# One attention and two MLPs on one core: the first MLP's weights loaded in step with their conversion, and chunk 1's Y transposed earlier

## The chip, the cores and the metric

One core of a Trainium2 chip runs the whole program in one launch. The metric is device time in microseconds (us). Engines are named as in the profile: PE (TensorE, with PEld for its weight loads), DVE (VectorE), ACT (ScalarE), POOL (GpSimd) and SP (SyncE, which here only issues DMAs).

## The reference

The inputs are q, k and v (4 x 8 x 768 x 48, float32), beta, and weights that reach the chip as 8-byte floats.

```python
for t in range(S):                       # per batch and head, k normalized
    y[:, :, t] = q[:, :, t] @ state      # read before the update
    state += beta[t] * outer(k[t], v[t] - state.T @ k[t])
x = y as 3072 x 384
h = x @ w_in                             # 384 x 2048
x = (max(h, 0) + alpha * min(h, 0)) @ w_out          # 2048 x 384
out = (silu(x @ w_gate) * (x @ w_val)) @ w_out2      # 384 x 1536, 1536 x 384
```

## The kernel before

**Stages.** The 768 time steps are cut into 24 chunks of 32. Attention of a chunk gives 128 rows of x (32 steps of 4 batches). The first MLP takes two chunks as one block (256 columns, 16 inner slices j, functions `H1`, `H1_parts`, `O1`), the second takes three. A `prelude` (lines 830 to 925) does chunks 0 and 1 by hand; everything after it is a list of events, each with a time in units, sorted and issued in that order. Each engine executes its own instructions in the order in which the program issued them.

**Attention.** `pre_T` transposes k or q on PE (ACT or DVE copies it out), `pre_G` makes the products of k and q, `lanes2(0)` inverts a triangular matrix for chunks 0 to 3, mostly on DVE. It begins with `norm` (line 218), whose first instruction is a square root on ACT (line 222) that DVE waits for. Then follow for each chunk `do_KS`, `do_QS`, `do_U`, `do_S`, `do_Y` and `do_XT`: small matmuls with one copy or sum behind each. `do_Y` copies Y out on ACT (`ys`, line 475); `do_XT` transposes it on PE and ACT and DVE write its two parts (`xh`, `xl`, lines 491 and 492). `H1` of block 0 needs `do_XT` of chunks 0 and 1.

**Weights of the first MLP.** There are 32 slices, 384 KB each; even ones are from w_in, odd ones from w_out. Each slice has a home in SBUF. `Slice.load` issues its DMA on SP. `all_w1` (line 797) is a generator that converts the slices, three steps for each slice: at step z=0 of slice i ACT reads slice i+2 (line 519, this waits for that slice's DMA), DVE does the first of three bit operations on slice i (lines 527, 529, 533, one a step), and ACT copies the upper part of slice i-1 (line 540). At z=1 the lower part of slice i-1 is subtracted (line 541), on POOL for the first 16 slices. The converted halves are written over the home of the slice. The float32 form lives in 8 tiles that the x tiles lend at first, then in 4 rotating ones, each free after the subtraction. `go(conv, n)` runs n steps: 3, then `C_A` = 6, `C_B` = 8, `C_C` = 9, 3, 3, `C_D` = 7, 2, 3 and 3 in the prelude, 47 steps in all; 50 more are events spread over units -0.5 to 13.5 of block 0.

**SP's queue before.** In this order: k of window 0 (4 DMAs), slices 0 to 4, q of window 0 (4), slice 5, k of window 1 (4), alpha, k of chunk 0 (4), slices 6 to 11, beta, slices 12 to 15, k of chunk 1, q of window 1 (waits for PE to have read k of window 1), slices 16 to 25, v of chunk 2, slices 26 to 31. None of the slices waits for the conversion.

Of the kernel before, what the change touches and what calls it, by code (L numbers as in the profile page):

```python
# [8 lines left out]
F32 = mybir.dt.float32  # L9
# [15 lines left out]
def kernel(  # L25
# [25 lines left out]
    nc = tc.nc  # L51
# [8 lines left out]
    J1 = FF1 // 128  # L60
# [5 lines left out]
    NB2 = NCH // CB2  # L66
    LA = 2
    W1_DVE = 16
    W64 = 1
    WF = 4  # L70

# [28 lines left out]
    def load_nat(w, nm, to, eng=nc.sync):  # L100

        src = {"k": k, "q": q}[nm]
        for b in range(4):
            eng.dma_start(
                out=to[b // 2][:, :, b % 2, 0:D],
                in_=src[b, :, w * 128:w * 128 + 128, :].rearrange("h t d -> t h d"),
            )
# [3 lines left out]
    def load_beta(w, eng=nc.sync):  # L111
        t = ap.tile([128, C], F32, name="beta", tag="beta", bufs=1)
        for b in range(4):
            eng.dma_start(
                out=t[32 * b:32 * b + 32],
                in_=beta[b, :, w * 4 * C:(w + 1) * 4 * C].rearrange("h (c t) -> c h t", c=4),
            )
        beta_t[w] = t
# [5 lines left out]
    def load_k2(c, eng=nc.sync):  # L124
        load_steps(k2_t[c % 2][:, 0 : H * D].rearrange("p (h d) -> p h d", h=H), k, c, eng)
# [3 lines left out]
    def load_v(c, eng=nc.sync):  # L129
        t = ap.tile([128, H, D], F32, name="v", tag="v", bufs=2)  # L130
        load_steps(t, v, c, eng)
        v_t[c] = t
# [7 lines left out]
    def bank(early, name):  # L140
        pool, tag = (ps_h1, "h1") if early else (ps_a, "a")
        return pool.tile([128, 512], F32, name=name, tag=tag)
# [272 lines left out]
    def do_QS(c):  # L415
        y_ps[c] = ps_y.tile([128, 512], F32, name="py", tag="y")
        if c > 0:
            state_rows(y_ps[c], c, 1, False)
# [61 lines left out]
    def do_XT(c):  # L480
        n, ci = divmod(c, 2)
        if ci == 0:
            x1_t[n] = [x1.tile([128, NK, N1], F32R, name=f"x{s}", tag=f"x{s}") for s in ("h", "l")]
        xh, xl = x1_t[n]
        ys = ys_t.pop(c)
        ps = bank(False, "px")
        for kk in range(NK):
            nc.tensor.transpose(ps[:, kk * 128:kk * 128 + 128], ys[:, kk * 128:kk * 128 + 128], ident)
        pv = ps[:, 0:NK * 128].rearrange("p (k t) -> p k t", k=NK)
        cs = slice(ci * 128, ci * 128 + 128)  # L490
        nc.scalar.activation(out=xh[:, :, cs], in_=pv, func=AF.Copy)  # L491
        nc.vector.tensor_tensor(xl[:, :, cs], pv, xh[:, :, cs], ALU.subtract)  # L492


    class Slice:
# [8 lines left out]
        def load(self, eng=nc.sync):  # L504
# [3 lines left out]
            else:  # L508
                if self.home is None:
                    w = wstg.tile([128, 384], I64, name="w64", tag="w64", bufs=W64)  # L510
                else:
# [25 lines left out]
    def split(f, eng, pool, tag):  # L537

        t = pool.tile([128, 2, 384], F32R, name="w", tag=tag, **({} if pool is ws else dict(bufs=1)))
        nc.scalar.activation(out=t[:, 0], in_=f, func=AF.Copy)  # L540
        return t, lambda: eng.tensor_tensor(t[:, 1], f, t[:, 0], ALU.subtract)  # L541
# [9 lines left out]
    for s in ("h", "l", "h", "l"):  # L551
        t = x1.tile([128, NK, N1], F32, name="ef" + s, tag="x" + s).rearrange("p k t -> p (k t)")
# [3 lines left out]
    def w1_slice(i):  # L556
        j, z = divmod(i, 2)
        src, parts = (w_rows(moe_w_out, j), 1) if z else (w_cols(moe_w_in, j), NK)

        wide = src.dtype == I64  # L560
        return Slice(src, parts, ws.tile([128, 384], I64, name="w64", tag="w") if wide else None)

    w1_s = [w1_slice(i) for i in range(2 * J1)]
# [222 lines left out]
    def warm(n, t=ident[:, 0:96]):  # L786

        if not warm_t:
            warm_t.append(ps_o1.tile([128, 2, 512], F32, name="warm", tag="o1"))
        for _ in range(n):  # L790
            nc.tensor.matmul(warm_t[0][0:96, 0, 0:96], t, t, start=True, stop=True)

    def load_w1(*slices, eng=nc.sync):
        for i in slices:
            w1_s[i].load(eng)

    def all_w1():


        n = 2 * J1  # L800
        rest = None
        for i in range(-2, n + 1):
            if i + 2 < n:
                w1_s[i + 2].act()
            if i < 0:
                continue
            for z in range(3):
                if i < n:
                    w1_s[i].dve(z)
                if z == 0 and i > 0:  # L810
                    t, rest = split(w1_s[i - 1].f, nc.vector if i >= W1_DVE and i % 2 else nc.gpsimd, ws, "w")
                    w1.append(t)
                if z == 1 and rest:
                    rest()
                if i < n or z == 1:
                    yield

    conv = all_w1()

    def go(g, n=1):  # L820
        for _ in range(n):
            next(g, None)
# [7 lines left out]
    def prelude():  # L830
        nc.vector.memset(St[:, 0, 0:2, :], 0.0)
        for z in range(2):
            nc.vector.memset(nat[z][:, :, :, D:64], 0.0)
        for z in range(2):
            nc.vector.memset(k2_t[z][:, H * D :], 0.0)
        nc.vector.memset(mask[:, 0:1], 1.0)
        nc.scalar.activation(out=mask[:, 1:2], in_=mask[:, 0:1], func=AF.Sqrt)
        make_identity(nc, ident)
        for z in range(2):
            nc.gpsimd.memset(natq0[z][:, :, :, D:64], 0.0)  # L840
        nc.gpsimd.memset(mask, 1.0)
        for g in range(4):
            m = mask[32 * g:32 * g + 32, :]
            nc.gpsimd.affine_select(
                out=m, in_=m, pattern=[[1, C]], compare_op=ALU.is_gt, fill=0.0, base=0, channel_multiplier=-1
            )
        load_nat(0, "k", nat)
        load_w1(0, 1, 2, 3, 4)
        load_beta(0, nc.gpsimd)
        load_v(0, nc.gpsimd)  # L850
        load_v(1, nc.gpsimd)
        warm(4, St[:, 0, 0:2, :].rearrange("p h e -> p (h e)"))
        n = 0
        for b1 in range(2):
            for half in range(2):
                pre_T(0, "k", b1, half, nat, early=n % 2 == 1, eng="act" if n % 2 == 0 else "dve")
                n += 1
        load_nat(0, "q", natq0)
        load_w1(5)
        load_nat(1, "k", nat)  # L860
        nc.sync.dma_start(out=alpha_r, in_=moe_alpha.rearrange("(j p) -> j p", p=128))
        load_k2(0)
        load_w1(*range(6, 12))
        go(conv, 3)
        for c in range(4):
            pre_G(c, (0,), early=c % 2 == 1)
        go(conv, C_A)
        inv = lanes2(0, True)
        go(inv, 3)
        load_beta(1)  # L870
        n = 0
        for b1 in range(2):
            for half in range(2):
                pre_T(0, "q", b1, half, natq0, early=n % 2 == 1)
                n += 1
        go(inv, 6)
        pre_G(0, (1,))
        go(inv, 2)
        pre_G(1, (1,), early=True)
        pa = bank(False, "pal")  # L880
        nc.tensor.transpose(pa[:, 0:J1], alpha_r, ident[0:J1, 0:J1])

        c = slope[:, 0]
        nc.vector.tensor_scalar(c, pa[:, 0:J1], -1.0, 1.0, op0=ALU.mult, op1=ALU.add)
        nc.vector.tensor_scalar(slope[:, 1], c, 0.0, 2.0, op0=ALU.is_ge, op1=ALU.mult)
        nc.vector.tensor_scalar(slope[:, 1], slope[:, 1], -1.0, None, op0=ALU.add)
        nc.vector.tensor_tensor(c, c, slope[:, 1], ALU.mult)
        nc.vector.tensor_scalar(c, c, -1.0, None, op0=ALU.mult)
        go(inv, 2)
        scale_v(0)  # L890
        scale_v(1)
        for b1 in range(2):
            for half in range(2):
                pre_T(1, "k", b1, half, nat)
        load_w1(*range(12, 16))
        load_k2(1)
        load_nat(1, "q", nat)
        load_w1(*range(16, 26))
        warm(6)
        go(inv, 7)  # L900
        go(inv)
        go(conv, C_B)
        go(inv)
        do_QS(0)
        do_U(0)
        go(conv, C_C)
        do_S(0)
        load_v(2)
        load_w1(*range(26, 2 * J1))
        go(conv, 3)  # L910
        do_KS(1)
        go(conv, 3)
        do_Y(0)
        do_QS(1)
        do_U(1)
        go(conv, C_D)
        do_XT(0)
        go(conv, 2)
        do_Y(1)
        go(conv, 3)  # L920
        do_S(1)
        load_k2(2)
        go(conv, 3)
        do_XT(1)
        return inv

    def base(c):
# [7 lines left out]
    for w in range(1, NWIN):  # L935
        P = base(4 * w) - 32
        if w == 1:
# [8 lines left out]
            l0, l1, n = 11.8, 23.6, LANES  # L946
        else:
# [9 lines left out]
            l0, l1, n = P + 15, P + 31.5, LANES  # L957
# [115 lines left out]
```

## Time and profile before

| | |
|---|---|
| device time, three runs | 1125.52, 1126.56 (median), 1130.23 us |
| profiled execution | span 1123.7 us from first to last instruction; its own device time is not listed beside it |
| busy | PE 1069.2, DVE 612.2, ACT 412.1, POOL 338.2 us |
| mean granted TensorE clock | 0.971 |
| moved by DMA | 76.40 MB, of which instructions 2.06 MB on one queue (126 packets) and 0.28 MB on another |

The page cuts the span into 40 slices of 28 us; a digit is a busy share in tenths. A row of a timeline is: start, duration, engine, line, operation, output and inputs, count, and in brackets how long the engine was idle before it and what released it ("issue": nothing that the profile shows). The chain of waits lists start and duration of the work that ended last.

### The profile page before, as it was taken

Reading aid. Unit: us, or ns where it says so; the run is one execution under the profiler, and the core shown is the slowest. Engines: PE = TensorE matmul, PEld = TensorE weight load, DVE = VectorE, ACT = ScalarE, POOL = GpSimd, SP = SyncE. Lnnn points to the kernel's source line nnn. Section 1 sums busy time; section 2 is a strip of 40 time slices with the busy share of each in tenths; the row PEclk is TensorE's granted clock in tenths of the full one; section 3 lists DMA queues with packets and bytes.
Section 4 is the critical chain, followed back from the end, with each engine's and each line's share of the span. In section 5 each row is a group of like instructions: output and inputs, shape, how many; then the busy total and the mean of one; then the engine's idle time right before and its main releaser. Section 6 shows DMA issues by size and latency. Waiting matters only on the chain.

```text
span 1123.7 us, 36882 instructions
## 1 busy us (share of the span) xinstructions
PE 1069.2 (95%) x16125; PEld 1038.2 (92%) x16125; DVE 612.2 (54%) x1314; ACT 412.1 (37%) x965; POOL 338.2 (30%) x521
## 2 busy tenths in 40 slices
PE   5559899999999999999999999999999999999998
PEld 4549788999999999999998999999999999999998
DVE  5867983974795497469544354433333333333333
ACT  3346343345434434533433564322222222222222
POOL 4334562742473274347322452100000000000000
PEclk8569999999999999999999999999999999999999
DMA  9941032405334240521333343010101010101000
GB/s 198 294 134 32 11 73 66 95 13 140 89 59 119 83 95 21 152 68 31 93 101 103 116 138 92 2 41 2 42 1 42 1 42 2 42 1 42 1 22 22
DMA packets 140196, 76.40 MB, mean 68 GB/s; under 512 B 104036, under 2 KB 134788, under 8 KB 140036
## 3 DMA queue, kind: packets, MB, share of 16 engines
q1 hardware_dynamic: 139460, 73.45, 25.3%
q8 instruction: 126, 2.06, 0.8%
q0 software_dynamic: 384, 0.41, 0.1%
q14 instruction: 34, 0.28, 0.1%
q10 hardware_dynamic: 192, 0.20, 0.1%
HBM read 57.52 MB, written 16.52 MB: 66 GB/s over the span
## 4 chain that ended last, share of the span: by engine, by line
PE 85%; DVE 6%; issue 4%; DMA 2%; ACT 1%; POOL 1%; SPq 0%; DVEq 0%; ACTq 0%; POOLq 0%
PE gv L696 27%; PE o L637 17%; PE h L606 16%; PE o L726 13%; PE pg L171 2%; PE pst L445 2%; PE pk L400 1%; PE pu L426 1%; PE pt L152 1%; PE py L466 1%; PE py L400 1%; POOL w L541 1%; DVE X L269 1%; DMA w<-in_moe_w_val_dram 1%; DMA w<-in_moe_w_out_dram 1%
## 5 line engine op out<-in xcount | busy, mean ns | idle before, releaser
L696 PE MATMUL gv<-x2s,w 128*128 128x384 f32 x1728 | 316.4, 335 | 0.0
L696 PEld LDWEIGHTS gv<-x2s,w 128*128 128x128 f32 x1728 | 303.2, 188 | 0.0
L606 PE MATMUL h<-xh,w 128*128 128x256 f32 x1152 | 242.5, 287 | 9.6 <-DVE pn L617 5.2
L637 PE MATMUL o<-gh,w 128*128 128x256 f32 x1728 | 247.6, 289 | 0.1
L626 POOL TENSOR_TENSOR gh<-pn,gh 128x256 fp32r<-128x256 f32 x192 | 155.3, 809 | 284.7 <-ACT gh L625 231.4
L637 PEld LDWEIGHTS o<-gh,w 128*128 128x128 f32 x1728 | 218.5, 190 | 5.4 <-DVE xs L652 0.3
L606 PEld LDWEIGHTS h<-xh,w 128*128 128x128 f32 x1152 | 193.0, 191 | 12.7 <-ACT xh L491 5.7
L606 PE MATMUL h<-xl,w 128*128 128x256 f32 x576 | 164.0, 285 | 2.6 <-DVE xl L492 2.6
L726 PE MATMUL o<-w,us 128*128 128x384 f32 x864 | 165.0, 336 | 0.0
L617 DVE SCALAR_TENSOR_TENSOR pn<-pn,slope,h 128x256 f32<-128x256 f32 x192 | 91.2, 475 | 121.2 <-ACT pn L616 120.8
L726 PEld LDWEIGHTS o<-w,us 128*128 128x128 f32 x864 | 151.2, 188 | 0.0
L708 DVE TENSOR_TENSOR sg<-sg,gv 128x384 f32<-128x384 f32 x96 | 53.2, 554 | 166.4 <-ACT sg L706 166.4
L625 ACT ACTIVATE gh<-pn 128x256 fp32r<-128x256 f32 x192 | 80.0, 417 | 131.2 <-DVE pn L617 129.7
L616 ACT ACTIVATE pn<-h,slope 128x256 f32<-128x256 f32 x192 | 90.0, 469 | 84.8 <-PE h L606 84.4
L606 PEld LDWEIGHTS h<-xl,w 128*128 128x128 f32 x576 | 110.3, 192 | 3.5 <-DVE xl L492 3.5
L681 POOL TENSOR_TENSOR x2s<-x2r,x2s 128x384 fp32r<-128x384 f32 x21 | 21.0, 1029 | 307.5 <-ACT x2s L679 307.5
L713 ACT ACTIVATE us<-u 128x384 fp32r<-128x384 f32 x96 | 50.5, 526 | 164.7 <-DVE u L709 164.7
L706 ACT ACTIVATE sg<-gv 128x384 f32<-128x384 f32 x96 | 47.3, 492 | 160.2 <-PE gv L696 160.1
L714 DVE TENSOR_TENSOR us<-u,us 128x384 fp32r<-128x384 f32 x96 | 53.6, 559 | 62.5 <-ACT us L713 62.5
L709 DVE TENSOR_TENSOR u<-sg,gv 128x384 f32<-128x384 f32 x96 | 53.2, 554 | 46.1 <-PE gv L696 46.1
L269 DVE TENSOR_TENSOR X<-X,tmp 128x31 f32<-128x31 f32 (+29 forms) x155 | 68.1, 439 | 4.8
L519 ACT ACTIVATE wf<-w 128x384 f32<-128x384 f32 x60 | 33.1, 552 | 84.4 <-DMA w<-in_moe_w_out_dram 27.3
(116 smaller groups left out, 1012.5 us busy)
## 6 DMA issues: line engine op xcount, KB each, us to landing
w<-in_moe_w_out_dram SPq DMA_DIRECT2D x28, 384.0 KB
w2d<-wf SPq DMA_DIRECT2D x36, 192.0 KB
wf<-w2d SPq DMA_DIRECT2D x36, 192.0 KB
w<-in_moe_w_in_dram SPq DMA_DIRECT2D x16, 384.0 KB
nat<-in_k_dram SPq DMA_DIRECT2D x24, 192.0 KB
k<-in_k_dram SPq DMA_DIRECT2D x96, 48.0 KB
x2d<-xs SPq DMA_DIRECT2D x12, 384.0 KB
w<-in_moe_w_gate_dram SPq DMA_DIRECT2D x12, 384.0 KB
```

What stands on the lines that cost most here:

```text
L269: eng.tensor_tensor(Xv, Xv, w, ALU.subtract)
L606: nc.tensor.matmul(ps[:, 0:N1], w[:, a, kk * 128:kk * 128 + 128], x[b][:, kk, :], start=(i == 0), stop=(i == 3 * NK - 1),)
L616: nc.scalar.activation(out=g, in_=hv, func=AF.Relu, scale=slope[:, 0, j:j + 1])
L617: nc.vector.scalar_tensor_tensor(out=g, in0=g, scalar=slope[:, 1, j:j + 1], in1=hv, op0=ALU.mult, op1=ALU.add)
L625: nc.scalar.activation(out=gh[:, 0], in_=g, func=AF.Copy)
L626: nc.gpsimd.tensor_tensor(gh[:, 1], g, gh[:, 0], ALU.subtract)
L637: nc.tensor.matmul(o[:, dm // 2, (dm % 2) * N1:(dm % 2) * N1 + N1], w[:, a, dm * 128:dm * 128 + 128], g[:, b], start=(j == 0 and i == 0 an ...
L696: nc.tensor.matmul(p[:, 0:N2], w2[j, z][:, a, kk * 128:kk * 128 + 128], x[:, b, kk], start=(i == 0), stop=(i == 3 * NK - 1),)
L708: nc.vector.tensor_tensor(sg, sg, ps[0], ALU.mult)
L709: nc.vector.tensor_tensor(u, sg, ps[1], ALU.mult)
L714: nc.vector.tensor_tensor(us[:, 1], u, us[:, 0], ALU.subtract)
L726: nc.tensor.matmul(o2_t[n][t][:, 0:DM], us[:, a, t * 128:t * 128 + 128], w[:, b, :], start=(j == 0 and i == 0), stop=(j == J2 - 1 and i == 2),
```

## The change

A constant `W1_AHEAD` = 6 is new. In the prelude only slices 0 to 5 are still loaded by hand: 0 to 2 behind k of window 0, 3 behind q of window 0, 4 and 5 behind k of chunk 0. Every other slice is loaded by the generator: at step z=1 of slice i, behind the subtraction of slice i-1, POOL sets 8 bytes per partition of the home of slice i+5, and SP issues its load, which has to wait for that POOL instruction. All SP work that the program issues later stands behind it. In the last part of the prelude, `do_S(1)`, the load of k of chunk 2 and `do_XT(1)` now come ahead of the six conversion steps that stood behind `do_Y(1)`.

```diff
+    W1_AHEAD = 6
...
                 if z == 1 and rest:
                     rest()
+                    if i - 1 + W1_AHEAD < n:
+                        t = w1_s[i - 1 + W1_AHEAD]
+                        if t.wide:
+                            nc.gpsimd.memset(t.home.bitcast(F32)[:, 0:2], 0.0)
+                        t.load()
...
         load_nat(0, "k", nat)
-        load_w1(0, 1, 2, 3, 4)
+        load_w1(0, 1, 2)
...
         load_nat(0, "q", natq0)
-        load_w1(5)
+        load_w1(3)
         load_nat(1, "k", nat)
         nc.sync.dma_start(out=alpha_r, in_=moe_alpha.rearrange("(j p) -> j p", p=128))
         load_k2(0)
-        load_w1(*range(6, 12))
+        load_w1(4, 5)
         go(conv, 3)
...
                 pre_T(1, "k", b1, half, nat)
-        load_w1(*range(12, 16))
         load_k2(1)
         load_nat(1, "q", nat)
-        load_w1(*range(16, 26))
...
         load_v(2)
-        load_w1(*range(26, 2 * J1))
         go(conv, 3)
...
         do_Y(1)
-        go(conv, 3)
         do_S(1)
         load_k2(2)
-        go(conv, 3)
         do_XT(1)
+        go(conv, 6)
```

## Rows read from the trace of the kernel before

**Rows 1.** Page, 40 slices of the span: PE's busy share in tenths
```profile
PE   5559899999999999999999999999999999999998
```

**Rows 2.** Chain of waits, 0 to 190 us: start, us, what
```profile
11.77 5.11 issue
...
20.80 1.48 DVE smr L223
...
43.22 1.08 POOL w L541
...
49.49 0.84 POOL w L541
```

**Rows 3.** Windows: length; busy PE, PEld, DVE, ACT, POOL; clock, DMA share, GB/s
```profile
38.99:42.50 3.51, 0.01 (x2) 0.01 (x1) 3.41 (x5) 1.67 (x4) 2.27 (x2) 0.50 0.84 136
...
52.10:53.42 1.32, 0.00 (x1) 0.00 (x1) 1.29 (x3) 0.52 (x1) 1.32 (x2) 0.50 1.05 386
57.38:60.71 3.33, 0.00 (x2) 0.00 (x0) 3.12 (x7) 0.00 (x0) 0.04 (x1) 0.50 1.14 275
67.50:74.50 7.00, 2.28 (x45) 1.47 (x38) 6.58 (x13) 3.67 (x9) 3.71 (x4) 0.55 0.26 50
```

**Rows 4.** Timeline of PE, 36 to 75 us
```profile
46.87 1.17 PE L426 MATMUL pu<-v,TT 32*32 32x48 f32 x43 [1.50 <-issue]
...
60.71 1.17 PE L400 MATMUL py<-St,kqt 48*32 48x48 f32 x44 [3.33 <-issue]
61.81 1.50 PE L426 MATMUL pu<-v,TT 32*32 32x48 f32 x64
```

**Rows 5.** Windows from 81 to 157 us, same columns as rows 3
```profile
81.25:90.00 8.75, 8.74 (x339) 8.10 (x339) 5.35 (x10) 2.72 (x7) 2.97 (x3) 0.61 0.01 4
...
118.00:157.00 39.00, 34.33 (x484) 32.16 (x483) 36.56 (x88) 15.20 (x40) 26.79 (x53) 0.96 0.21 43
```

**Rows 6.** Timeline of ACT, 47 to 77 us
```profile
51.03 0.47 ACT L460 ACTIVATE St<-pst 128x384 f32<-128x384 f32 x1
...
56.17 0.47 ACT L475 ACTIVATE ys<-py 128x384 f32<-128x384 f32 x1
...
68.75 0.47 ACT L475 ACTIVATE ys<-py 128x384 f32<-128x384 f32 x1
...
73.16 0.46 ACT L491 ACTIVATE xh<-px 128x384 fp32r<-128x384 f32 x1
...
76.39 0.48 ACT L616 ACTIVATE pn<-h,slope 128x256 f32<-128x256 f32 x1 [0.92 <-PE h L606]
```

**Rows 7.** Timeline of ACT, 17 to 29 us
```profile
19.11 0.56 ACT L519 ACTIVATE efh<-w 128x384 f32<-128x384 f32 x1
...
20.50 0.27 ACT L222 ACTIVATE sms<-L 128x32 f32<-128x32 f32 x1 [0.42 <-DVE L L207]
```

**Rows 8.** Timeline of SP's queue, 0 to 200 us
```profile
6.89 9.96 SPq L104 DMA_DIRECT2D natq<-in_q_dram  x4
...
25.89 0.45 SPq L514 DMA_DIRECT2D w<-in_moe_w_in_dram  x1
...
178.02 0.38 SPq L514 DMA_DIRECT2D w<-in_moe_w_val_dram  x1
```

**Rows 9.** Windows of 10 us, same columns as rows 3
```profile
0.00:10.00 10.00, 5.84 (x56) 4.93 (x58) 1.82 (x9) 3.33 (x8) 8.20 (x24) 1.00 0.96 199
10.00:20.00 10.00, 4.89 (x251) 4.71 (x243) 6.19 (x13) 3.79 (x10) 1.65 (x3) 0.68 0.99 241
```

**Rows 10.** Chain of waits, 540 to 600 us: loads of the same size
```profile
557.44 3.23 DMA w<-in_moe_w_gate_dram
...
586.07 4.59 DMA w<-in_moe_w_val_dram
```

**Rows 11.** Timeline of DVE, 37 to 78 us
```profile
44.21 0.42 DVE L377 TENSOR_TENSOR TT<-TT,pi 128x256 f32<-128x256 f32 x1 [0.76 <-PE pi L368]
```

**Rows 12.** Timeline of PE, 157 to 192 us
```profile
182.42 0.54 PE L400 MATMUL py<-St,kqt 48*32 48x48 f32 x30 [1.05 <-issue]
```

## The prediction

> **What bounds the kernel now.** I read the page's 40 slices first, then the chain of waits up to 190 us, then the engines' timelines along that chain. In the page the reader sees PE idle for half of the first three slices and full from the fourth on [rows 1]. So the change can act only on the head. What it wins or loses there is carried along if the stretches behind it are paced by work that starts as much earlier or later.
>
> Head to 74 us. The chain begins with k's DMA, its transposes and products, then a pause of PE without a releaser, 11.77 to 16.88, and goes on through ACT's square root into DVE's `smr` at 20.80 and the inversion [rows 2]. Behind it come the small matmuls of chunks 0 and 1. There PE pauses again without a releaser: 3.51 us up to 42.50, 1.50 up to 46.87, 1.32 up to 53.42, 3.33 up to 60.71. Where a window shows such a pause, the DMA share is 0.84 to 1.14; the window from 67.50, with 45 matmuls, has a share of 0.26 and no such pause [rows 3, 4]. PE's instructions come by DMA too. From 46.87 to 52.10 PE did 127 matmuls and as many weight loads, about 254 instructions, and then stood. I read these pauses as instruction fetches queued behind the weights.
>
> From 81 us PE is busy nearly all the time, at a clock of 0.61 up to 90; from 118 to 157 DVE is, 36.56 of 39.00 us [rows 5]. DVE's part begins when PE's events reach it, so it too starts earlier or later with the head.
>
> **The change part by part.** I follow one number, how much later (+) or earlier (-) than in the trace a milestone comes, down to the first H1 evacuation (`pn` on ACT, 76.39 [rows 6]).
>
> *Slice 4 is late for ACT, +6.5.* ACT reads slice 4 at 19.11, in the conversion step before `lanes2`; one more conversion instruction, 0.45 us behind it, and then the square root at 20.50, which waited 0.42 us for DVE [rows 7]. That order on ACT stays, so the root now waits for slice 4. Today slice 4 is issued ahead of q. After the change it stands on SP behind q, k of window 1 and k of chunk 0, where slice 6 stands today, issued at 25.89; SP was held up before that, as the 9.96 us for four DMAs of q show [rows 8]. Two slices fewer stand ahead of it. They are 0.79 MB, at 241 GB/s 3.3 us [rows 9], so slice 4 is issued near 22.6. Loads of this size land 3.23 to 4.59 us after issue [rows 10]: 25.8 to 27.2. ACT reads it at 26.1 and takes the root 0.9 us later, at 27.0. The lower end is by bytes alone: 4.92 MB stand up to the end of slice 4 (three times 0.79 of k and q, five slices of 0.39, 0.20 and 0.39 of k and v), and 1.99 and 2.41 MB had moved by 20 us [rows 9]; the rest needs 2.2 us more, root at 23.2, a shift of 2.7. The upper end is 7.6. I take 6.5, nearest the order on SP. DVE waits for the root and then has the same work, so the inversion is late by as much. The first pause, 11.77 to 16.88, no longer decides, whether it shrinks or not.
>
> *Pauses of PE go, -0.8, -1.9, -3.6.* One slice now loads for each that ACT and POOL convert in turn, 0.39 MB in about 2.2 us (0.56 and 0.52 on ACT, 1.08 on POOL [rows 2, 7]), 180 GB/s against 386 in the fullest window [rows 3]: the DMA engines are about half busy. I take it that the pauses then vanish; the other end is that they stay as they are. The 3.5 us before 42.50 are worth only 0.8, because DVE converts until 43.45 and then waited 0.76 us for PE [rows 11]: +5.7. `pu` could start at 44.63 and ended at 48.04; it needs 1.50 [rows 4, 11]: U of chunk 0 stands at +3.8.
>
> *ACT waits for slices 10 and 11, +1.3.* Slice 10's load now follows the subtraction of slice 4 on POOL, in the trace at 43.22, and slice 11's that of slice 5, at 49.49 [rows 2]. Slice 10 is issued near 51.0 (43.22 plus 1.1, 0.2 and the 6.5 us) and lands at 54.5, where ACT comes to it at 53.9: `St` (51.03 [rows 6]) at +4.4. Slice 11 is issued near 54.7 (ACT's half of slice 5 follows U) and lands near 58.3, while ACT is free at 55.9. ACT has three conversion parts more until `ys`, with one wait for POOL between, 2.9 us: `ys` at 61.3 (56.17 [rows 6]), +5.1. PE has `py` ready at 59, so the 1.32 us of the pause in `pk` are lost in this wait. If loads need 4.6 us it is 1 more; if slices 10 and 11 land in time, it is -1.3 in place of +1.3.
>
> *QS of chunk 1 without its pause, -3.6.* `py` could start at 56.64 and ended at 61.88; such 64 matmuls need 1.5 [rows 4, 6], and 1.6 is taken: U of chunk 1 at +1.5. From here to `ys` of chunk 1 (68.75) ACT converts at the pace of ACT and POOL in turn, which is kept; what PE does beside it is hidden.
>
> *XT of chunk 1 ahead of six steps, -2.9.* `xh` came 4.41 us behind `ys` (68.75 to 73.16 [rows 6]); without the two slices between them PE's three transposes and ACT's start need 1.5: -1.4. The two slices are now converted while H1 of j = 0 and 1 runs; ACT needs 3.4 us for them and comes to `pn` 0.2 us later behind `xh` than today's 3.23: -1.2. DVE has the same work in all, and idles less.
>
> *Block 0, +1.0.* Twelve loads, 4.7 MB, now fall between 74 and 115 us, where the DMA share was 0.01 up to 90 [rows 5]. Their slack is eight steps, some 8 us against 4.59, so no conversion waits. But the trace has a PE pause of 1.05 us without a releaser up to 182.42, 4.4 us after the issue of a single weight load [rows 8, 12]. Ends: 0 and 3 us; I take one such pause, since the PE-bound stretch would carry it. The 26 memsets of 8 bytes find room: POOL was busy 2.97 of 8.75 us [rows 5].
>
> Sum: 6.5 - 0.8 - 1.9 + 1.3 - 3.6 - 2.9 + 0.2 + 1.0 = -0.2 us. The profiled span is 1123.7 us, 2.9 us under the median of the three runs, which I take as what lies around it. The median less 0.2: 1126.4 us.
>
> **The rivals.** *The pauses stay (slower).* Place: PE's fetches from 38 to 67 us, and beside each load up to 115 us. It holds if they come from the fetch itself and not from the weights, and decides once the pauses that ended at 42.50 and 60.71 both keep 2 us or more. Then -0.8, -1.9 and -3.6 are gone, and the waits for slices 10 and 11 (1.3) hide behind the pauses: +4.8, and with two pauses in block 0 instead of one +5.8: 1131.4 to 1132.4 us. For it: one load beside a fetch may do what many do [rows 12]. Against it: no pause from 67.50 on, when the weights are all in [rows 3]. The Trainium skill, DMA: Bandwidth & Descriptors, section Queues, rings and completion order, says that a DMA engine takes its queue rows in turn, a packet at a time. By that rule a fetch on its own queue does not stand behind the whole backlog of weights, and this rival, 1131.4 to 1132.4, is the likelier. The trace speaks against the strong form of the rule, with pauses of 1.32 to 5.11 us beside full engines, but cannot show which part of a pause is queueing.
>
> *Slice 4 is in time (faster).* If SP lets q and k through sooner than its backlog suggests, ACT waits 2 us or less and the sum is 4.5 smaller, 1121.9; with no wait at all and slices 10 and 11 in time too, 6.5 and 2.6 smaller, 1117.3. For it: the lower end by bytes. Against it: the order on SP, which the slice cannot pass.
>
> *The loads don't fall into step.* If the loads bunch as today, pauses stay and only slice 4's delay and XT's gain are left: 6.5 - 2.9 + 0.2, 1130.4.
>
> *Loads too late in block 0.* If a load takes over 8 us from POOL's memset, ACT stands at every slice with H1's evacuations behind it: 17 slices at 1 us, 1143. No load in the rows is that slow.
>
> **How the numbers follow.** The forecast, a change of a few us either way: 0.52. The pauses stay 0.19, slice 4 in time 0.22, not in step 0.04, block 0 late 0.03. A measurement of this kernel can tell 0.5%, 5.6 us, from no change: faster means under 1120.9, slower over 1132.2. The forecast's own range is from 2.7 instead of 6.5 with half of the waits for slices (-5) to half of the pauses kept and slow loads (+5): 1121 to 1131.5. Faster: most of the second rival and a tail of the forecast, among others a clock that rises before 90, 0.24. Slower: half of the first rival, the last, and a tail, 0.20. The range of 8 in 10 is 1118.5 to 1132.5.
>
> **What would show it.** ACT waits some 6 us for a DMA at line 519 before the root, and `smr` comes near 27 instead of 20.80; PE's pauses after 38 us are under 1 us; ACT waits for slices 10 and 11 at about 54 and 56 us; `xh` of chunk 1 comes 1.5 us behind `ys`; H1 starts near 72. Wrong would be the root before 23, or pauses over 2 us beside a DMA share of one half.

## The result, and the profile after

The changed kernel is slower: 1135.38 us, median of 6 runs (1131.76 to 1138.72), against 1126.71 us for the kernel before beside it (1123.9 to 1130.23). The ratio is 1.0076, 95% interval 1.0053 to 1.0099. That is 8.7 us where -0.2 was forecast, and above the range. The profiled execution took 1137.12 us with a span of 1135.3, so in the two profiles there are 11.6 us to account for. The new constant moves the line numbers behind it up by one: the ACT read of a slice is L520 (L519 before), the square root L223 (L222). L819 is the new memset on POOL.

PE's 40 slices on the page after [rows 1]:

```profile
PE   4559888999999999999998999999999999999998
```

The first slice is a tenth emptier, and three later ones (the sixth and seventh, 142 to 199 us, and the 22nd) are no longer full. The chain of waits (start, us, what) says what came into it:

```profile
22.82 4.13 DMA w<-in_moe_w_in_dram
28.11 1.86 DVE smr L224
...
120.85 2.59 issue
```

The reader sees a weight load, slice 4, ahead of `smr`, which came at 20.80 before [rows 2], and a pause of PE that stands in block 0, where there was none of that size. Why slice 4 came so late is in SP's timeline:

```profile
5.85 6.43 SPq L105 DMA_DIRECT2D natq<-in_q_dram  x4
...
14.79 3.49 SPq L105 DMA_DIRECT2D nat<-in_k_dram  x4
18.33 2.50 SPq L867 DMA_DIRECT2D alpha_r<-in_moe_alpha_dram  x1
20.87 1.90 SPq L123 DMA_DIRECT2D k<-in_k_dram  x4
22.82 0.45 SPq L515 DMA_DIRECT2D w<-in_moe_w_in_dram  x1
...
116.12 0.35 SPq L515 DMA_DIRECT2D w<-in_moe_w_out_dram  x1
116.57 3.38 SPq L105 DMA_DIRECT2D nat<-in_k_dram  x4
```

SP is held at q, k and alpha, and issues slice 4 at 22.82 (forecast: 22.6). The last two rows matter below: the last slice leaves at 116.12, and k of window 2 follows directly.

ACT's timeline after; to be read beside [rows 6, 7]:

```profile
26.97 0.55 ACT L520 ACTIVATE efh<-w 128x384 f32<-128x384 f32 x1 [8.24 <-DMA w<-in_moe_w_in_dram]
27.83 0.24 ACT L223 ACTIVATE sms<-L 128x32 f32<-128x32 f32 x1
...
55.90 0.56 ACT L520 ACTIVATE wf<-w 128x384 f32<-128x384 f32 x1 [0.67 <-DMA w<-in_moe_w_in_dram]
...
58.79 0.57 ACT L520 ACTIVATE wf<-w 128x384 f32<-128x384 f32 x1 [1.55 <-DMA w<-in_moe_w_out_dram]
61.65 0.55 ACT L520 ACTIVATE wf<-w 128x384 f32<-128x384 f32 x1 [1.80 <-DMA w<-in_moe_w_in_dram]
62.51 0.47 ACT L476 ACTIVATE ys<-py 128x384 f32<-128x384 f32 x1
67.29 0.49 ACT L436 ACTIVATE U<-pu 128x384 f32<-128x384 f32 x1 [4.30 <-PE pu L427]
72.67 0.47 ACT L476 ACTIVATE ys<-py 128x384 f32<-128x384 f32 x1
74.13 0.49 ACT L492 ACTIVATE xh<-px 128x384 fp32r<-128x384 f32 x1 [0.99 <-PE px L489]
74.52 0.54 ACT L520 ACTIVATE wf<-w 128x384 f32<-128x384 f32 x1
75.71 0.52 ACT L541 ACTIVATE w<-wf 128x384 fp32r<-128x384 f32 x1 [0.65 <-DVE wf L534]
77.50 0.57 ACT L520 ACTIVATE wf<-w 128x384 f32<-128x384 f32 x1 [1.27 <-POOL w L819]
77.97 0.52 ACT L541 ACTIVATE w<-wf 128x384 fp32r<-128x384 f32 x1
79.72 0.56 ACT L520 ACTIVATE wf<-w 128x384 f32<-128x384 f32 x1 [1.23 <-POOL w L819]
80.18 0.51 ACT L541 ACTIVATE w<-wf 128x384 fp32r<-128x384 f32 x1
80.59 0.46 ACT L617 ACTIVATE pn<-h,slope 128x256 f32<-128x256 f32 x1
```

The reader sees four things: 8.24 us of waiting for slice 4 ahead of the root; three shorter DMA waits, for slices 10, 11 and 12; `xh` 1.46 us behind `ys`; and three whole slices (a read and a copy each) between `xh` and `pn`. That stretch is 6.46 us long; it was 3.23.

PE's timeline after [rows 4, 12]:

```profile
46.69 0.51 PE L369 MATMUL pi<-tmp,Dm 16*32 16x16 f32 x22 [0.55 <-issue]
47.50 1.67 PE L369 MATMUL pi<-tmp,Dm 16*32 16x16 f32 x106 [0.30 <-issue]
...
64.62 1.17 PE L401 MATMUL py<-St,kqt 48*32 48x48 f32 x44 [0.89 <-issue]
...
68.83 0.98 PE L467 MATMUL py<-U,mt 32*32 32x48 f32 x47 [0.24 <-issue]
...
120.34 0.50 PE L172 MATMUL pg<-kqt 48*32 48x64 f32 x20
123.44 0.94 PE L172 MATMUL pg<-kqt 48*32 48x64 f32 x44 [2.59 <-issue]
...
128.05 1.10 PE L172 MATMUL pg<-kqt 48*32 48x64 f32 x64
```

The pauses without a releaser between 38 and 72 us shrank to four, 1.98 us in sum; before there were six, 11.78 us, of which [rows 4] shows two. But a pause of 2.59 us stands at 120.85. In the kernel before, the same matmuls of `pg` are these:

```profile
115.38 0.50 PE L171 MATMUL pg<-kqt 48*32 48x64 f32 x20
116.10 0.86 PE L171 MATMUL pg<-kqt 48*32 48x64 f32 x44 [0.22 <-issue]
...
119.21 1.10 PE L171 MATMUL pg<-kqt 48*32 48x64 f32 x64
```

PE is 4.96 us late ahead of the pause (120.34 against 115.38), 7.34 behind it and 8.84 at the next `pg`. Windows after, columns as in [rows 3, 5]:

```profile
50.00:60.00 10.00, 4.68 (x184) 4.33 (x188) 9.76 (x17) 5.13 (x11) 4.60 (x9) 0.50 0.65 191
118.00:120.85 2.85, 2.85 (x137) 2.48 (x125) 2.75 (x9) 1.15 (x4) 0.07 (x1) 1.00 1.30 237
120.85:123.44 2.59, 0.00 (x1) 0.00 (x1) 0.54 (x2) 0.66 (x2) 1.66 (x2) 1.00 1.09 124
123.44:128.00 4.56, 4.56 (x62) 4.30 (x61) 1.75 (x4) 1.30 (x3) 0.00 (x0) 0.63 0.02 5
```

The DMA share is 1.30 in the 2.85 us ahead of the pause and 1.09 in it. Behind it the granted clock is 0.63, a mean between the levels of 1.2 and 2.4 GHz, and that makes the step from 7.34 to 8.84.

The 11.6 us of the two profiles are then: 4.45 in the head (PE at 81 us), 0.5 up to the pause, 2.4 the pause, 1.5 the clock behind it, 0.3 up to `py` at 182.42 [rows 12], which now comes at 191.56, and 2.45 behind that.

### The profile page after: what moved, and what is told of

It reads as the page before. It is cut to its first block, busy times and chain, and to the rows that moved or that the text cites. A ratio compares the mean times of both kernels' runs of the same rounds, so it can differ in the third digit from the quotient of the medians.

```text
span 1135.3 us, 36945 instructions
## 1 busy us (share of the span) xinstructions
PE 1074.0 (95%) x16125; PEld 1042.7 (92%) x16125; DVE 614.0 (54%) x1314; ACT 411.1 (36%) x965; POOL 338.4 (30%) x547
## 4 chain that ended last, share of the span: by engine, by line
PE 86%; DVE 6%; DMA 3%; issue 2%; ACT 1%; SPq 1%; POOL 1%; DVEq 0%; ACTq 0%; POOLq 0%
PE gv L697 27%; PE o L638 17%; PE h L607 16%; PE o L727 13%; PE pg L172 2%; PE pst L446 2%; PE pu L427 2%; PE pk L401 2%; PE py L401 2%; PE pt L153 1%; PE py L467 1%; DMA w<-in_moe_w_out_dram 1%; POOL w L542 1%; DMA w<-in_moe_w_in_dram 1%; DVE X L270 1%
## 5 line engine op out<-in xcount | busy, mean ns | idle before, releaser
L520 ACT ACTIVATE wf<-w 128x384 f32<-128x384 f32 x60 | 33.2, 553 | 95.3 <-DMA w<-in_moe_w_out_dram 33.4
```

## The experiments

My theory was that the loss is the late slice 4, the slices that now stand ahead of `pn`, and k of window 2 following the last slice as one burst. The rival was that loading in step itself costs: waits and pauses beside each load. Each run stands beside runs of the kernel before on the same chip; ratios are to those.

**E1: the change, with slice 4 early again.**

```diff
-load_w1(0, 1, 2)
+load_w1(0, 1, 2, 3, 4)
 ...
-load_w1(3)
+load_w1(5)
 ...
-load_w1(4, 5)
```

> The changed kernel with slices 0 to 4 issued ahead of q and slice 5 behind q, as before the change; slices 6 to 31 still in step, chunk 1's transposes still early. Theory A (the loss is slice 4: in the changed kernel ACT stood 8.24 us for its load and the square root came at 27.83 instead of 20.50): the root is back at 20 to 21, the 7.3 us are gone from everything up to 115 us, H1 starts near 67 to 69, and the time falls by 5 to 8 us from the changed kernel's 1135.4, to 1127 to 1130. Theory B (in-step loads themselves hold the conversion, so that slices 10 to 12 and the ACT-POOL alternation set the end of the head): the root is early, but the first H1 evacuation stays within 2 us of its 80.59, and the time stays above 1133.

Measured: 1130.27 us against 1125.16, ratio 1.0032 (1.0019 to 1.0045). ACT's timeline of E1, and the window of the pause in block 0:

```profile
21.28 0.26 ACT L223 ACTIVATE sms<-L 128x32 f32<-128x32 f32 x1 [0.43 <-DVE L L208]
...
55.14 0.55 ACT L520 ACTIVATE wf<-w 128x384 f32<-128x384 f32 x1 [2.10 <-DMA w<-in_moe_w_in_dram]
...
66.43 0.49 ACT L492 ACTIVATE xh<-px 128x384 fp32r<-128x384 f32 x1 [0.64 <-PE px L489]
72.88 0.46 ACT L617 ACTIVATE pn<-h,slope 128x256 f32<-128x256 f32 x1
```

```profile
114.25:116.58 2.33, 0.00 (x0) 0.00 (x0) 0.54 (x2) 0.65 (x2) 1.66 (x2) 1.00 1.22 138
```

The root is back at 21.28 and the loss falls from 0.76% to 0.32%, some 5 us: slice 4 is the largest part. Three things stay: ACT's waits for slices 10 to 12, 6.45 us from `xh` to `pn`, and the pause (2.33 us at a DMA share of 1.22). PE is 3.2 us ahead of the kernel before at 81 us and 5.5 behind at the end; 3.6 us of this turn are the pause and the slower clock behind it.

**E3: the kernel before, with slices 3, 4 and 5 at the places that the change gives them.**

```diff
-load_w1(0, 1, 2, 3, 4)
+load_w1(0, 1, 2)
 ...
-load_w1(5)
+load_w1(3)
 ...
-load_w1(*range(6, 12))
+load_w1(*range(4, 12))
```

> The kernel before with only slices 3, 4 and 5 moved to their new places on SP (3 behind q, 4 and 5 behind k of chunk 0, then 6 to 11 at once); nothing is in step, the transposes stay late. Theory A (slice 4's place is the loss, and DVE has no idle time between the root and St of chunk 0 that could take it up): ACT waits some 8 us at line 519, the root comes at 27 to 28, the pauses of PE from 38 to 67 us are still there, and the time is 5 to 8 us above 1126.7: 1132 to 1135. Rival (the delay would be absorbed by PE's pauses, which end when the fetches land and not when the root comes): under 1129.

Measured: 1132.64 us against 1125.16, ratio 1.0053 (1.0035 to 1.007). ACT's timeline of E3:

```profile
27.24 0.54 ACT L519 ACTIVATE efh<-w 128x384 f32<-128x384 f32 x1 [8.21 <-DMA w<-in_moe_w_in_dram]
28.11 0.24 ACT L222 ACTIVATE sms<-L 128x32 f32<-128x32 f32 x1
```

The same wait, with nothing else of the change, costs 0.53%, 6 us or a little more. E1 and E3 are the two sides of one cause.

**E2: the kernel before, with chunk 1's transposes ahead of the six steps.**

```diff
 do_Y(1)
-go(conv, 3)
 do_S(1)
 load_k2(2)
-go(conv, 3)
 do_XT(1)
+go(conv, 6)
```

> The kernel before with only the order at the end of the prelude changed: S(1), the load of k of chunk 2 and XT(1) ahead of the six conversion steps; all weights loaded as before. Theory A (the first H1 evacuation stands on ACT behind three slices' conversion whatever the order, since two more conversion steps follow in the event list): xh of chunk 1 comes some 3 us earlier (near 70), H1 starts near 70.7, but the evacuation stays within 1 us of 76.4 and the time within 2 us of 1126.7. Theory B, the prediction's step: evacuation 2.9 us earlier, time 1124.

Measured: 1127.81 us against 1125.16, ratio 1.0022 (1.0004 to 1.0039). ACT's timeline of E2:

```profile
65.31 0.47 ACT L475 ACTIVATE ys<-py 128x384 f32<-128x384 f32 x1
66.77 0.49 ACT L491 ACTIVATE xh<-px 128x384 fp32r<-128x384 f32 x1 [0.99 <-PE px L488]
...
73.21 0.47 ACT L616 ACTIVATE pn<-h,slope 128x256 f32<-128x256 f32 x1
```

From `ys` to `pn` it is 7.90 us; in [rows 6] it is 7.64 (68.75 to 76.39). `xh` comes sooner and `pn` doesn't: this half of the change earns nothing by itself.

**E10: E1 with the old order at the end of the prelude** (the diff of E2 backwards, on E1).

> e1 (in step, slices 0 to 4 first) with the end of the prelude in the old order: three conversion steps, S(1), three steps, XT(1). Theory A (the early transposes give nothing, since the first H1 evacuation stands behind the same conversion): xh of chunk 1 comes 4.4 us behind ys instead of 1.1, the evacuation 7 to 8 us behind ys as in e1, and the time is within 1.5 us of e1's 1130.3. Theory B (the prediction's step): evacuation and time 2 to 3 us later than e1, 1132 to 1133.

Measured: 1125.61 us against 1123.80, ratio 1.0014 (0.9996 to 1.0032). From `ys` (65.01) to `pn` (72.69) it is 7.68 us, in E1 7.56 (65.32 to 72.88), and PE's matmuls stand at most 0.54 us off E1's from 78 to 195 us and at most 0.9 us sooner up to 490. Behind that E10's profile gains 3 us more on E1's, for a reason that stays open. The intervals of E1 and E10 overlap. The moved transposes are worth nothing, from this side too.

**E4: the change, with k of window 2 three units later in the list of events.**

```diff
-at(P - 5, load_nat, w, "k", nat)
+at(P - 2 if w == 2 else P - 5, load_nat, w, "k", nat)
```

> The changed kernel with the load of k of window 2 three units later (unit 14 instead of 11), so that it no longer follows the last weight slice on SP at 116.57, where PE then stood 2.59 us at 120.85 beside a DMA share of 1.09 and went on at half clock. Theory A (that burst is 3 to 4 us of the loss): no such pause near 120, the time 1131 to 1133. Rival (the pause belongs to the fetch at this place in the code, or the burst only meets another fetch): a pause of over 1.5 us between 115 and 140 remains, the time 1134 to 1136.

Measured: 1135.98 us against 1125.16, ratio 1.0087 (1.0067 to 1.0106). The load still left SP right behind the last slice, at 117.72, and a pause of 2.33 us ended at 124.33. The edit changed nothing: SP had no other work between, so the later place in the list left the DMA where it was. This run says nothing on the burst; the next does.

**E5: E1, with two memsets of a few bytes on POOL that k of window 2 has to wait for.**

```diff
-at(P - 5, load_nat, w, "k", nat)
+if w == 2:
+    def gated(w=w):
+        for z in range(2):
+            nc.gpsimd.memset(nat[z][:, 0, :, 0:2], 0.0)
+        load_nat(w, "k", nat)
+    at(P - 1.5, gated)
+else:
+    at(P - 5, load_nat, w, "k", nat)
```

> Slices 0 to 4 first (as in e1), and window 2's k load now really later: in e4 it stayed right behind the last slice on SP, which runs ahead of the other engines, and the pause stayed with it. Here POOL writes 8 bytes of each nat tile at unit 14.5 and the load waits for that. Theory A (the burst of 4096 short rows takes the fetch of the block that starts with 44 of the pg matmuls: 2.33 us of pause and some 1.2 us at half clock behind it): no pause over 1 us between 110 and 120, and the time 3 to 4 us under e1's 1130.3: 1126 to 1128. Rival (the pause is the fetch's own, as the 0.83 us of e2 beside an idle DMA hint, or the burst meets another fetch): pause or a new one of 2 us stays, time within 1.5 us of 1130.3.

Measured: 1127.63 us against 1124.95, ratio 1.0007 (0.9992 to 1.0022), with one run of 5749.21 us left out of the ratio. The load leaves at 137.54. Windows of E5 at the same matmuls:

```profile
115.44:116.12 0.68, 0.01 (x2) 0.00 (x0) 0.56 (x2) 0.67 (x2) 0.68 (x1) 1.00 0.00 0
116.12:120.00 3.88, 3.88 (x117) 3.65 (x120) 2.10 (x5) 1.53 (x4) 1.01 (x2) 1.00 0.01 4
```

The pause is 0.68 us at an idle DMA, and the clock stays at 1.00 behind it. In the two profiles PE goes from 1.2 us behind E1 at 110 us to 2.0 ahead at 125. By the ratios the loss goes from 0.32% to 0.07%, some 2.8 us; the two intervals just overlap, so the times alone don't settle the size.

**E9: the change itself, with the memsets of E5.**

> The changed kernel itself with only window 2's k load held back by POOL to unit 14.5 (the gate of e5); slice 4 stays late. Theory A (the two losses add): the root stays at 27 to 28, the pause near 120 falls from 2.59 to under 1 us, the time is 2 to 4 us under the changed kernel's 1135.4, at 1131.5 to 1133.5. Rival (e5's gain came from its early slice 4 and a lucky set of runs): within 1.5 us of 1135.4.

Measured: 1131.53 us against 1123.80, ratio 1.0083 (1.0057 to 1.0109). The slices still load beside `pg` (the last one leaves at 116.94), k of window 2 leaves at 143.55, and the pause is 0.48 us instead of 2.59. In the profile PE goes from 0.8 us behind the change to 2.8 ahead at these matmuls, and the end comes 4.2 us sooner. But the ratio isn't lower than the change's 1.0076: the kernel before was 2.9 us faster in these runs too. With four runs the interval is 0.5% wide, so the time neither shows nor rules out such a gain; the trace confirms the mechanism.

**E6: the kernel before, profiled again.**

> The kernel before, unchanged, one more profile. In its first profile PE's pauses between 38 and 67 us came to 11.8 us (0.52, 3.50, 1.50, 1.32, 3.33, 1.61); in e2, whose loads are the same up to 62 us, to some 5.9. Theory A (the pauses vary from execution to execution, and the first profile was one of the larger ones): the sum here is between 4 and 9 us, and U of chunk 1 comes at 60 to 62 instead of 63.38. Rival (they are fixed by the order of the loads, so that e2's early transposes or its load of k of chunk 2 made the difference): the sum is again 11 to 12 us and U at 63 to 64.

Measured: one run, 1126.08 us. The six pauses of PE between 38 and 67 us add up to 9.4 us (0.52, 3.07, 1.23, 1.33, 2.50, 0.79), where the first profile has 11.78; E2, with the same loads, has 5.9. `pn` comes at 74.57 instead of 76.39. So the same program pauses more or less from one execution to the next, and the sizes that I took for them came from a long one.

**E7: E1, with slices loaded ten ahead instead of six.**

```diff
-W1_AHEAD = 6
+W1_AHEAD = 10
 ...
 load_k2(0)
+load_w1(6, 7, 8, 9)
```

> Slices 0 to 4 first (as in e1), and ten slices ahead instead of six: 6 to 9 are issued by hand behind k of chunk 0, slice i+9 by the step that took i+5. Theory A (in e1 ACT still waited 0.72, 1.50 and 2.10 us for slices 10, 11 and 12, and the last slice came so late on SP that window 2's k followed as one burst): no DMA waits of ACT at line 519/520 behind 22 us, ys of chunk 0 some 1 to 2 us earlier than e1's 56.0, window 2's k no longer a burst behind 105 us; time 1125 to 1128. Rival (the loads ahead bring PE's pauses of 38 to 67 us back, since more of them are on the way at once): pauses of over 3 us in sum there, time 1129 to 1132.

Measured: 1124.23 us against 1124.95, ratio 0.9996 (0.998 to 1.0011). ACT waits for no slice behind 15 us; `ys` of chunk 0 comes at 53.84 and not at 56.01 as in E1. k of window 2 leaves at 98.97, and the pause at `pg` is 0.34 us. So loading in step costs nothing once it is far enough ahead, which speaks against the rival. It gains nothing either: PE is 4.7 us ahead of the kernel before at 81 us, 2.9 at 182, 1.4 at 194, and level at 614. The step from 2.9 to 1.4 is a pause of 1.23 us at 191.21.

**E8: E7, with the six moved steps left to the events of block 0.**

```diff
 do_XT(1)
-go(conv, 6)
 ...
-CONV_DONE, CONV_END = 17 + sum(CONVS), 13.5
+CONV_DONE, CONV_END = 11 + sum(CONVS), 13.5
```

> e7 with the six conversion steps behind XT(1) taken out of the prelude and spread with the others over block 0 (56 steps from unit -0.5 to 13.5 instead of 50). Theory A (XT(1) ahead of the six steps gives nothing because H1's first evacuation still stands behind the conversion on ACT): now the evacuation comes 3 to 4 us behind xh of chunk 1 instead of 6.4, and 2 to 3 us earlier than in e7; the time falls by 1 to 3 us from e7's if PE and not DVE paces block 0. Rival (DVE, 36.6 of 39 us busy from 118 on, has the same work and gives it back): evacuation early, time within 1 us of e7's.

Measured: 1123.87 us against 1124.95, ratio 0.9984 (0.997 to 0.9997). ACT's timeline of E8, and DVE's stretch in a window of it:

```profile
65.85 0.49 ACT L492 ACTIVATE xh<-px 128x384 fp32r<-128x384 f32 x1 [0.99 <-PE px L489]
66.24 0.54 ACT L520 ACTIVATE wf<-w 128x384 f32<-128x384 f32 x1
67.43 0.52 ACT L541 ACTIVATE w<-wf 128x384 fp32r<-128x384 f32 x1 [0.65 <-DVE wf L534]
69.10 0.47 ACT L617 ACTIVATE pn<-h,slope 128x256 f32<-128x256 f32 x1 [1.15 <-PE h L607]
```

```profile
118.00:157.00 39.00, 31.02 (x344) 28.93 (x342) 37.03 (x89) 13.57 (x37) 27.86 (x56) 0.96 0.25 51
```

With one slice between them `pn` follows `xh` by 3.25 us, as before the change, and `pn` now waits for PE. This is what the early transposes needed. PE is 7.3 us ahead of the kernel before at 74 us, 5.7 at 130, 2.6 at 140 and level at 194. In the window DVE is busy 37.03 of 39 us and PE only 31.02, so I read the loss from 130 to 140 as DVE taking the lead back; the last 2 us go in a pause of PE, 1.79 us at 191.95. E8 is the one version whose interval lies below the kernel before, by 0.16%, 1.1 us between the medians.

## Why the prediction was wrong

How much later than in [rows 2, 6, 11] each milestone came, as the prediction put it and as the profile after has it:

| milestone | predicted | measured |
|---|---|---|
| `smr` (20.80) | +6.5 | +7.3 |
| TT (44.21) | +5.7 | +6.8 |
| `U` of chunk 0 (48.08) | +3.8 | +4.95 |
| `ys` of chunk 0 (56.17) | +5.1 | +6.3 |
| `U` of chunk 1 (63.38) | +1.5 | +3.9 |
| `ys` of chunk 1 (68.75) | +1.5 | +3.9 |
| `xh` of chunk 1 (73.16) | -1.4 | +1.0 |
| `pn` (76.39) | -1.2 | +4.2 |

**Slice 4: mechanism right, size 0.8 short.** Issue (22.82 for 22.6) and landing (4.13 us, inside 3.23 to 4.59 [rows 10]) came as worked out. The lower end by bytes and the rival "slice 4 is in time" are refuted. The order on SP decided.

**Pauses: gone as forecast, but worth less.** 11.78 us became 1.98, while the DMA share was 0.65 from 50 to 60 us; "the pauses stay" is refuted for the head. Between 38 and 72 us such pauses sum to 5.9 to 11.8 us wherever the loads aren't in step (the kernel before twice, E2, E3) and to 1.4 to 4.1 in the eight programs where they are. The first two gains came as written, nearly (-0.5 for -0.8, -1.85 for -1.9). QS of chunk 1 gave -2.4 instead of -3.6, because a pause of 0.89 us stayed at 64.62. And E6 shows that the baseline's pauses differ by 2 us between executions, so gains reckoned from one profile need not be in the median.

**Waits for slices: right, +1.4 for +1.3,** though there were three (0.67, 1.55 and 1.80 us) and I had named two. E7 takes them away, and `ys` comes 2.2 us sooner than in E1.

**The failing step: "comes to `pn` 0.2 us later".** `xh` moved by the 2.9 us as predicted. But I reckoned 3.4 us for the two moved slices alone and left out the one that stood between `xh` and `pn` all along. Three slices stand there, each at some 2.15 us, since ACT waits for POOL between them: 6.46 us, so the step costs 3.2 and not 0.2. That takes back the whole gain of the early transposes. E2 and E10 show that nothing is left, E8 that 3.25 us are enough without the two slices.

**The other failing step: "block 0, +1.0".** It came to 4.4: 0.5 up to 120.34, then the pause and its clock. I had priced a pause beside one weight load [rows 12]. What came was k of window 2: four DMAs of 192 KB in rows of 192 bytes, which had left SP at 97.20 before and now came behind the last slice. ACT waited for no slice from 74 to 120 us, as forecast. E5 and E9 take k of window 2 from its place, and the pause falls from 2.33 to 0.68 and from 2.59 to 0.48 us. It is this burst, not the slices in step, that makes the pause. Four runs have the burst at this `pg` (the change, E1, E4, E10), with pauses of 1.78 to 2.59 us; the eight others have 0.83 us at most.

Part of the rival's mechanism holds there: the fetch of PE's instructions does come late beside a full DMA. The traces show it. PE's instructions come as packets of 16 KB on the queue that the page calls `q8 instruction`, one for every 255 of PE's matmuls and weight loads, and up to 260 us every pause of 0.2 us or more without a releaser ends 1.1 to 1.8 us after such a packet did (but for two that have the same length in all twelve traces, 0.5 and 1.5 us). Over the 255 instructions ahead of this pause PE took 3.0 us, before and after the change. In the kernel before, the packet began 0.91 us after the first of them and took 1.00, and PE went on 1.29 us later; in the changed one these are 2.5, 1.46 and 1.60. So of the 2.4 us that the pause grew, 1.6 lie ahead of the packet and the rest in it and behind it. In the kernel before, the same four DMAs left at 97.20 beside a stretch in which PE took 8.3 us over 255 instructions, and it didn't pause there. The Trainium skill, Runtime: NRT & Kernel Launch, section Instruction fetch mechanics, says that crossing a block of instructions is mostly hidden; the trace agrees nearly at an idle DMA (0.22 us at 116.10 before, 0.83 in E2) and not at a share above 1 (2.59 us).

**What is left, 2.45 us behind 191 us,** I had not forecast at all. The chain of waits after shows one more such pause:

```profile
203.22 1.53 issue
204.75 0.41 PE pg L172 x12
```

PE is 9.14 us late ahead of it and 12.49 at 209.55: the pause, and a granted clock of 0.64 for the 4.75 us behind it. By the end 1.0 us of this came back. The packet began at 202.40 there, 3.1 us after a weight load left SP (199.32); in the kernel before it began 0.9 us after the same load (190.18), and PE didn't pause. That the load came first here is luck: E1, E3, E7, E8 and E10 have a pause at this place too, 0.42 to 1.79 us, and the other six traces have none of 0.2 us or more. Medians differ by 8.7 us and not by 11.6, so some 3 us belong to the two profiled executions. Why 1.0 us came back wasn't tried and stays open.

The misses add up: 0.8, 0.3, 1.2 and 3.0 in the head, with some 0.1 of rounding 5.4 us; 0.25 from `pn` to 81 us, 3.4 in block 0, 0.3 up to 182 and 2.45 behind it. That is 11.8, from the -0.2 of the forecast to the 11.6 of the profiles.

## What to carry to other kernels

When a DMA is moved on one queue, look up which engine's next instruction waits for it and what else stands behind that instruction: here one conversion read held back a square root and the whole head. When work is moved behind a step, count all of it that then stands ahead of the next step on that engine, not only what was moved. What a load costs depends on what is fetched beside it: the same four DMAs cost nothing beside long matmuls and 2.4 us beside short ones, where PE soon needed its next instructions, and then the slower clock.

## What the runs showed of the hardware

- A burst of four DMAs of 192-byte rows (share 1.09 to 1.48 in the pause) lengthened a pause of PE from at most 0.83 us to 1.78 to 2.59 us. At these matmuls the packet of PE's next 255 instructions began 0.91 us after PE had started on the 255 ahead of it with an idle DMA, and 2.5 us after it with the burst. Behind the pause of 2.59 the granted clock was 0.63 for 4.56 us; behind the one of 0.68 it was 1.00.
- An event's place in the program's list didn't time a DMA: moved by three units, it still left directly behind the one ahead of it (117.72). Two small memsets, which it had to wait for, moved it to 137.54.
- One program's pauses between 38 and 67 us added up to 11.78 us in one execution and 9.4 in another, with spans of 1123.7 and 1124.1 us: less pausing in the head didn't make the end come sooner. In the second PE was 1.8 us ahead at 81 us and 1.9 behind at 190; 2.4 us of this are a pause of 2.01 us up to 182.84 (1.05 in the first) and a clock of 0.63 behind it.
